# A block-sparse attention and MLP kernel: its planned issue order replaced by a written-out table

## The chip, the cores and the metric

One Trainium2 chip, one of its cores. The metric is the device time of one execution in microseconds (us). The kernel before took 760.85, 762.11 and 762.67 us in three runs, so its median is 762.11 us. A measurement of this kernel can tell a difference of about 0.2%, some 1.5 us, from no change.

## The reference

Four batches, eight heads, 768 positions, head size 64. Attention is restricted by blocks of 32 positions: a query block sees its own block and its two neighbours, the first and the last block, and three drawn blocks. The result is laid out as 3072 tokens of 512 and goes through two matrix products with a gate between them. The weights are float64 (512 by 2048 and 2048 by 512), q, k and v are float32.

```python
scores = np.where(mask, scale * q @ k.T, -1e9)
attn = softmax(scores)
x = (attn @ v).transpose(0, 2, 1, 3).reshape(3072, 512)
h = x @ w_in
g = h * np.tanh(np.log1p(np.exp(np.minimum(h, 20.0))))
out = g @ w_out
```

## The kernel before

Every float32 or float64 operand is brought to a common scale and split into two 16-bit halves, a high part and a low part, and every product is made of three matmuls (high-high, low-high, high-low).

**Weights.** The float64 weights come in as pairs of int32 words. VectorE turns them into float32 with three instructions for each of 8 pieces of w_in (`wi`) and 16 pieces of w_out (`wo`): `add_decode`, L901, L904 and L907. TensorE forms a sum of squares of each piece (`gram_wi`, `gram_wo`, L373), and the scale from it (`gsc`, L1029, for all of w_in) must be there before the first MLP product. `split_i` (L953) then makes the high half on ScalarE or VectorE (L962, L964) and the low half either on VectorE in one instruction (L968) or on GpSimd (POOL) in two (L971, L973).

**Attention.** 52 jobs, 13 for each batch; a job takes two query blocks (or one dense block that sees all keys). `attend` (L698) writes a job as a chain: S, the scores (TensorE, L674, 48 matmuls of 64x32 tiles when the gathered keys are whole, 96 in the first 12 jobs); the maximum (VectorE, L737); the exponentials (ScalarE); T, four transposes (TensorE, L680); the halves `ph` and `pl`; O, the product with v (TensorE, L818, 96 matmuls of 128x32 tiles, 144 in a dense job) into the one bank `obank`; the division by the sum (VectorE, `r` at L837 and `xs` at L840, which read `obank`); X, a transpose back (`tx`, L680, and L870 in the first six jobs); and the halves of x. GpSimd gathers the keys (`kg`, L611) and the SP queue the values (`vg`).

**MLP.** For 12 tiles of 256 tokens: h products (L1068, 12 matmuls to a half task), the gate on ScalarE, VectorE and GpSimd, y products (L1162). The last four tiles use a scheme with seven products instead of eight (L1281). A tile's h products need `gsc` and the x of all the jobs that cover its tokens. For the first tile, h of tile 0, these are jobs 0 to 4.

**The order.** The whole kernel is first listed as 2703 tasks (`Plan.add`, L76): a task names its engine or the engines it may run on, a duration, what it reads and writes, and the buffers it takes. `Plan.emit` (L124) then replays this list against assumed durations: at every step it takes the task that could start first, among those within 0.02 us by urgency (`URGE`, `JOBS`, `PIECES`, L33 to L35), picks an engine for tasks that have a choice, and issues its instructions. Each engine runs its own instructions strictly in the order of issue. `pace` (L1507) holds attention back on TensorE: set starting times for the first 14 jobs, a share of MLP work between jobs after that, and, after 200 us of planned time, at least 2.0 us of MLP work between any two S or O tasks:

```python
if kind in ("S", "O") and start > SPACE[0] and at["done"] < at["dense"] + SPACE[1]:
    late = max(late, SPACE[2])
```

`fill` (L1541) issues products of zeros into an unused part of `obank` (L1545, 240 columns) wherever the plan shows TensorE empty between 14 and 200 us, one for each 0.14 us, unless an O is half done. There are 176 of them.

Of the kernel before, what the change touches and what calls it, by code (L numbers as in the profile page):

```python
# [1 line left out]

# [62 lines left out]
class Plan:  # L65
# [55 lines left out]
                return at + dur if grain is True else min(at + dur, start + grain)  # L121
        return start

    def emit(self, pace, fill):  # L124


        for t in self.tasks:
            t.left = len(t.deps)
            for d in t.deps:
                d.then.append(t)  # L130
        free, ready, dma, held = {}, {}, {}, {}
        lanes = {w: [[0.0] * self.LANES, 0] for w in ("hard", "soft")}

        def open_(t):
            for e in t.ways:
                ready.setdefault(e, []).append(t)

        for t in self.tasks:
            if not t.left:
                open_(t)  # L140
        todo = len(self.tasks)
        self.order = []
        while todo:
            best = None
            load = {e: free.get(e, 0.0) + 0.5 * sum(t.ways[e][0] for t in ts if len(t.ways) == 1)
                    for e, ts in ready.items() if e != "PE"}
            for eng, ts in ready.items():
                f = free.get(eng, 0.0)
                cand = []
                for t in ts:  # L150
                    at, took = t.ready, []
                    for ring, k in t.new:
                        slot = self.room(ring, took)
                        if slot is None:
                            at = None
                            break
                        took.append((ring, slot[1], k))
                        at = max(at, slot[0])
                    if at is None:
                        continue  # L160
                    if len(t.ways) > 1:
                        done = {e: max(at, load.get(e, 0.0)) + x[0] for e, x in t.ways.items()}
                        if done[eng] > min(done.values()):
                            continue
                    if t.kind and t.kind[0] == "dma":
                        lane, n = lanes["soft" if eng == "POOL" else "hard"]
                        at = max(at, lane[n % self.LANES])
                    start = self.port(held, eng, max(at, f), t.ways[eng][2])
                    late, bias = pace(t, start) if eng == "PE" else (0.0, 0.0)
                    cand.append((start + late, t.ready + t.key + bias, t.n, start, t, took))  # L170
                if not cand:
                    continue
                lo = min(c[0] for c in cand)
                c = min((c[1:] for c in cand if c[0] <= lo + 0.02), key=lambda c: c[:2])
                if best is None or c[2] < best[0]:
                    best = *c[2:], eng
            start, t, took, t.eng = best
            for e in t.ways:
                ready[e].remove(t)
            t.dur, fn, port = t.ways[t.eng]  # L180
            if port:
                held[t.eng] = start, t.dur, port
            t.fill = fill(free.get("PE", 0.0), start) if t.eng == "PE" else 0
            end = start + t.dur + (pace(t, None) or 0.0)
            free[t.eng] = end
            if t.kind and t.kind[0] == "dma":

                lane, n, end, t.end = *lanes["soft" if t.eng == "POOL" else "hard"], start, 0.0
                each = t.kind[1] / t.kind[2]
                for k in range(n, n + t.kind[2]):  # L190
                    end = max(end, lane[k % self.LANES]) + t.dur / t.kind[2]
                    other = max([x for e, x in dma.items() if e != t.eng], default=0.0)
                    at = max(dma.get(t.eng, 0.0), end + 0.3)
                    dma[t.eng] = at + each + min(each, 0.5 * max(other - at, 0.0))
                    lane[k % self.LANES] = land = max(dma[t.eng] + 0.5, end + t.lat + min(max(other - end, 0.0), 3.5))
                    t.end = max(t.end, land)
                lanes["soft" if t.eng == "POOL" else "hard"][1] += t.kind[2]
                free[t.eng] = end
            else:
                t.end = end + t.lat  # L200
            t.at = start
            for ring, slot, k in took:
                self.rings[ring][slot] = k
            fn()
            todo -= 1
            self.order.append(t)
            for x in t.then:
                x.left -= 1
                x.ready = max(x.ready, t.end + self.SEM if x.eng != t.eng or t.kind and t.kind[0] == "dma" else t.end - t.lat)
                if not x.left:  # L210
                    open_(x)


def edges(nb, gpc):
# [5 lines left out]
def attn_mish_kernel(ctx: ExitStack, tc: tile.TileContext, qT, kT, v, sampled, blocks, w_in, w_out, out):  # L220
# [13 lines left out]
    B, NPR, D2, S = qT.shape  # L234
# [108 lines left out]
    plan = Plan(RINGS)  # L343
# [843 lines left out]
    dma = lambda d, n=1: ("dma", d, n)  # L1187
# [156 lines left out]
    for b in range(B):  # L1344
        order = [(0,)] + [(q, q + 1) for q in range(1, NB - 1, 2)]
        order.insert(DL, (NB - 1,))
        for qbs in order:
            sus = [{"b": b, "qb": qb} for qb in qbs]
            dense = len(qbs) == 1
            jobs.append({"i": len(jobs), "b": b, "sus": sus, "dense": dense, "nt": S // KT if dense else len(qbs)})  # L1350
    nj = len(jobs)
# [52 lines left out]
    for k in range(NFP):  # L1404
# [3 lines left out]
        key=-9)  # L1408

    order = []  # L1410
# [21 lines left out]
    for i, job in enumerate(jobs):  # L1432
        b, o = job["b"], i % JB
# [61 lines left out]
    for st in order[len(plain):] + [None]:  # L1495
        steps, end = pair_y(prev, st is None)
        ys = [(0.66, x) for x in steps[:-1]] + [(0.66, lambda s_=steps[-1], e=end: (s_(), e()))]
        mixed([(2.62, lambda n=n, st=st: moe_h(st, n, None)) for n in range(NFP)] if st else [], ys)
        prev = st
    total = sum(t.ways["PE"][0] for t in plan.tasks if t.kind and t.kind[0] == "M")  # L1500

    RES, START = 575.0, [26, 134, 14, 98, 36, 170, 29, 37, 53, 110, 67, 166, 3, 46]
    at = {"done": 0.0, "next": 0.0, "job": 0, "last": None, "shape": None, "open": False, "dense": -9.0}

    SPACE = 200.0, 2.0, 1.5

    def pace(t, start):  # L1507

        kind = t.kind[0] if t.kind else None
        if start is None:  # L1510
            shape = 0.0
            if t.eng == "PE":
                now = kind if kind in ("S", "O") else None
                shape, at["shape"] = 0.1 * (now != at["shape"]), now
                if kind == "M":
                    at["done"] += t.dur
                elif kind == "S":
                    at["job"] += 1
                    at["next"] = at["done"] + max(total - at["done"] - RES, 0.0) / max(nj - at["job"], 1)
                elif kind == "O":  # L1520
                    at["open"] = not t.kind[2]
                at["last"] = kind
                if kind in ("S", "O"):
                    at["dense"] = at["done"]
            return shape
        if kind == "M":
            return 0.0, 1e6 - t.ready + t.kind[1] - t.key
        late = 0.0
        if kind == "S":
            i = t.kind[1]  # L1530
            if i < len(START):
                late = max(START[i] - start, 0.0)
            elif at["done"] < at["next"]:
                late = 1.0
        if kind in ("S", "O") and at["last"] in ("S", "O") and kind != at["last"]:
            late = max(late, 0.3)
        if kind in ("S", "O") and start > SPACE[0] and at["done"] < at["dense"] + SPACE[1]:
            late = max(late, SPACE[2])
        return late, 0.0

    def fill(a, b):  # L1541

        n = int((b - a - 0.15) / 0.14) if FILL[0] < a < FILL[1] and not at["open"] else 0
        for _ in range(n):
            nc.tensor.matmul(obank[:, NO:NO + NZ], neg[:, 0], neg.rearrange("p n q -> p (n q)")[:, 0:NZ],  # L1545
                             start=True, stop=True)
        return max(n, 0)

    FILL = 14.0, 200.0
    plan.emit(pace, fill)  # L1550
    pools["lcm"].__exit__(None, None, None)
    pools["cm"].__exit__(None, None, None)


# [40 lines left out]
```

## Time and profile before

| | |
|---|---|
| median of three runs | 762.11 us (760.85 to 762.67) |
| the profiled execution, first to last instruction | 760.4 us |
| TensorE busy | 718.7 us (95%), 13086 matmuls |
| VectorE busy | 580.0 us (76%) |
| ScalarE busy | 575.1 us (76%) |
| GpSimd busy | 350.7 us (46%) |
| products of zeros, L1545 | 26.2 us, 176 of them |

The profiled execution is told by its span of 760.4 us; its time with what lies around the span is not given apart, and the median of the runs is 1.7 us above it. The engines are PE (TensorE), PEld (its weight loads), DVE (VectorE), ACT (ScalarE), POOL (GpSimd) and SP. "issue" marks time in which an engine waited for nothing that the profile shows. [...]

### The profile page before, as it was taken

The page shows a single profiled execution, that of the slowest core. Times are in us where ns is not written, and L with a number is a line of the kernel's source. Part 1 is how long each engine was busy: PE and PEld are TensorE (multiplying, and loading weights), DVE is VectorE, ACT ScalarE, POOL GpSimd, SP SyncE. Part 2 cuts the span into 40 slices and gives each one's busy share as a digit, 9 for nine tenths or more (in the row PEclk, how much of TensorE's full clock was granted, in tenths as well). Part 3 has the DMA queues.
Part 4 walks back from the last instruction along what each step waited for, and adds up shares of the span by engine and source line. Part 5 has one row for each costly group of instructions (what it writes and reads, how often), then busy time and mean ns, then how long its engine had stood idle before and what let it go on. Part 6 is the DMA issues. An engine that isn't in the chain of part 4 may idle for free.

```text
span 760.4 us, 31382 instructions
## 1 busy us (share of the span) xinstructions
PE 718.7 (95%) x13086; PEld 546.5 (72%) x13086; DVE 580.0 (76%) x1007; ACT 575.1 (76%) x905; POOL 350.7 (46%) x415
## 2 busy tenths in 40 slices
PE   5867789999999999999999999999999999999997
PEld 4746677775686777776776667667676778888886
DVE  4989878999878766789777866988775765777674
ACT  3566668889788788879788779787887877677762
POOL 2055744536956444545436642558773511421110
PEclk9998899999999999999999999999999999999999
DMA  9688766543334466174246643733541446000000
GB/s 332 221 273 227 245 198 180 169 107 100 122 95 144 123 184 195 54 222 143 71 117 192 189 136 89 228 100 89 155 129 45 121 115 230 28 2 28 1 27 31
DMA packets 60050, 103.76 MB, mean 136 GB/s; under 512 B 8579, under 2 KB 20868, under 8 KB 59908
## 3 DMA queue, kind: packets, MB, share of 16 engines
q1 hardware_dynamic: 53616, 86.28, 37.9%
q10 hardware_dynamic: 6292, 15.47, 5.9%
q8 instruction: 103, 1.69, 0.9%
q14 instruction: 39, 0.32, 0.1%
HBM read 84.58 MB, written 17.14 MB: 134 GB/s over the span
## 4 chain that ended last, share of the span: by engine, by line
PE 73%; DVE 16%; DMA 5%; issue 2%; ACT 2%; SPq 2%; POOL 1%; DVEq 0%; POOLq 0%; ACTq 0%
PE h_None L1068 25%; PE y L1162 18%; PE yr L1281 8%; PE t L680 6%; PE obank L818 5%; PE s L674 5%; DVE wo L907 2%; PE tx L680 2%; DMA vg<-vd 1%; PE obank L1281 1%; DMA raw_q<-in_q_dram 1%; PE obank L1545 1%; DVE v L504 1%; DVE fr_o L1201 1%; DVE hs_None L1107 1%
## 5 line engine op out<-in xcount | busy, mean ns | idle before, releaser
L1068 PEld LDWEIGHTS <-wi 128*128 128x128 f16 x2304 | 222.8, 98 | 32.4 <-issue 2.5
L1068 PE MATMUL h_None<-xh,wi 128*128 128x256 f16 x1152 | 207.2, 273 | 0.0
L611 POOL COPY kg<-kt 128x256 f16 x255 | 125.7, 527 | 121.6 <-PE s L674 110.8
L1162 PE MATMUL y<-wo,g 128*128 128x512 f16 x672 | 160.9, 379 | 1.0 <-DVE wo L1025 0.8
L1068 PE MATMUL h_None<-xl,wi 128*128 128x256 f16 x576 | 157.0, 273 | 0.0
L1120 POOL TENSOR_TENSOR g<-hs_None,g 128x1024 f16<-128x1024 f32 x36 | 85.0, 2363 | 93.0 <-ACT g L1114 49.9
L1162 PEld LDWEIGHTS <-g 128*128 128x128 f16 x768 | 73.0, 98 | 73.2 <-issue 3.6
L756 ACT ACTIVATE pt<-s,nb,ns 128x256 f32<-128x256 f32 (+1 forms) x208 | 106.2, 583 | 1.1
L1079 ACT ACTIVATE hs_None<-h_None,gsc 128x512 f32<-128x512 f32 x96 | 65.4, 684 | 36.6 <-PE h_None L1068 34.1
L783 DVE SCALAR_TENSOR_TENSOR pl<-t,ph 128x512 f16<-128x512 f32 x99 | 67.0, 685 | 32.7 <-ACT ph L779 32.2
L1107 DVE SCALAR_TENSOR_TENSOR hs_None<-us_None,hs_None 128x1024 f32<-128x1024 f32 x48 | 62.5, 1305 | 28.7 <-ACT us_None L1106 28.6
L779 ACT ACTIVATE ph<-t 128x512 f16<-128x512 f32 x112 | 65.6, 598 | 24.1 <-PE t L680 23.6
L680 PE MATMUL t<-ident,pt 128*128 128x128 f32 x448 | 70.1, 283 | 8.3 <-DVE sc_q L409 3.0
L1103 POOL TENSOR_TENSOR us_None<-us_None 128x1024 f32<-128x1024 f32 x24 | 47.9, 1997 | 53.6 <-DVE us_None L1101 53.6
L1068 PE MATMUL h_None<-xr,wi 128*128 128x256 f16 x576 | 66.5, 273 | 0.0
L680 PEld LDWEIGHTS t<-ident,pt 128*128 128x128 f32 x448 | 51.9, 143 | 20.2 <-issue 8.8
L737 DVE TENSOR_REDUCE mx<-s 128x4 f32<-128x1024 f32 x44 | 53.6, 1219 | 16.4 <-PE s L674 16.2
L818 PEld LDWEIGHTS <-ph 128*32 128x32 f16 x3584 | 48.0, 94 | 19.5 <-issue 14.9
L1098 ACT ACTIVATE us_None<-hs_None,hsc 128x1024 f32<-128x1024 f32 x48 | 55.0, 1147 | 0.3
L1105 ACT ACTIVATE us_None<-us_None 128x1024 f32<-128x1024 f32 x48 | 50.7, 1055 | 2.7 <-POOL us_None L1103 2.3
L818 PE MATMUL obank<-vg,ph 128*32 128x65 f16 (+1 forms) x3200 | 50.6, 196 | 1.4 <-issue 1.2
L1106 ACT ACTIVATE us_None<-us_None 128x1024 f32<-128x1024 f32 x48 | 50.4, 1055 | 0.7
(260 smaller groups left out, 1279.4 us busy)
## 6 DMA issues: line engine op xcount, KB each, us to landing
vg<-vd SPq DMA_DIRECT2D x320, 65.0 KB, 2.7
vg<-vd SPq DMA_DIRECT2D x80, 195.0 KB, 3.1
wr<-in_moe_w_in_dram ACTq DMA_DIRECT2D x8, 1024.0 KB, 7.3
wor<-in_moe_w_out_dram ACTq DMA_DIRECT2D x13, 512.0 KB, 6.1
vd<-v SPq DMA_DIRECT2D x12, 520.0 KB, 3.1
vg<-vd SPq DMA_DIRECT2D x12, 520.0 KB, 4.9
raw_k<-in_k_dram SPq DMA_DIRECT2D x12, 512.0 KB, 5.4
raw_q<-in_q_dram SPq DMA_DIRECT2D x12, 512.0 KB, 4.7
```

Of the source, the lines that this page charges most:

```text
L611: nc.gpsimd.tensor_copy(out=dst, in_=tl["kt", b][:, :, ds(j, BS)])
L680: nc.tensor.matmul(out, src, ident, start=start, stop=stop, is_transpose=True)
L756: ex = lambda o, x, g, w: nc.scalar.activation(out=o, in_=x, func=AF.Exp, bias=nb[:, g, w:w + 1], scale=tl["ns", b, sus[w]["qb"] // TB][:, ...
L779: nc.scalar.activation(out=new(at_, "ph", ("ph", i, j), [P, 2, 2, P], F16), in_=tl["t", i, j], func=AF.Copy, scale=PSC)
L783: nc.vector.scalar_tensor_tensor(out=new(at_, "pl", ("pl", i, j), [P, 2, 2, P], F16), in0=tl["t", i, j], scalar=PSC, in1=tl["ph", i, j], o ...
L818: nc.tensor.matmul(o[cs, w, g, 0:v1 - v0], p[:, k, g, cs], vt[:, k, 2 * c + g, v0:v1], start=j == 0 and g == 0 and k == 0 and n == 0, stop ...
L1068: nc.tensor.matmul(h[:, f2, 0:n].rearrange("p (s q) -> p s q", q=BS), wi[:, fp, w, cc, fs], x[:, s0:s0 + sn, cc], start=f2 == 0 and k == 0 ...
L1079: nc.scalar.activation(out=tl[kq][:, 2 * (fp % 2):2 * (fp % 2) + 2, 0:n], in_=tl[kh][:, :, 0:n], func=AF.Copy, scale=gsc[:, fp:fp + 1])
L1107: add("DVE", 1.32 * c, lambda: nc.vector.scalar_tensor_tensor(out=hs(), in0=us(), scalar=-0.5, in1=hs(), op0=ALU.add, op1=ALU.mult), r=[ku ...
L1120: add("POOL", 2.3 * c, lambda: nc.gpsimd.tensor_tensor(out=g(1), in0=hs(), in1=g(0), op=ALU.subtract), r=[kq, ("gh",) + kp], w=[kp], use=[kg],
L1162: nc.tensor.matmul(tl[ky], tl["g", b, t, k][:, g, f, q], wo_at(fc)[:, w], start=fc == 0 and n == 0, stop=fc == NFC - 1 and n == 2)
L1281: nc.tensor.matmul(R(i), lhs, rhs, start=head and j == n == 0, stop=k == NFC // 4 - 1 and j == 1 and n == 2, skip_group_check=True)
```

## The change

The list scheduler, its times and its pacing rules are taken out. The order stands in a string of 2703 words, `ORDER`; a word is a task's number, a letter where it runs on another than its first engine, and the count of zero products to issue ahead of it. `emit` issues the tasks in that order. The tasks themselves, their instructions and their dependencies are the same.

```diff
-    def emit(self, pace, fill):
...
+    def emit(self, order, fill):
+        done = set()
+        self.order = []
+        for word in order.split():
+            n, way, zeros = re.fullmatch(r"(\d+)([b-z]?)(?:\+(\d+))?", word).groups()
+            t = self.tasks[int(n)]
+            t.eng = list(t.ways)[ord(way) - 97 if way else 0]
+            assert t not in done and t.deps <= done, "the order puts a task before one that it needs"
+            fill(t, int(zeros or 0))
+            t.ways[t.eng][1]()
+            done.add(t)
             self.order.append(t)
...
-    SPACE = 200.0, 2.0, 1.5
-    def pace(t, start):
...
-    def fill(a, b):
-        n = int((b - a - 0.15) / 0.14) if FILL[0] < a < FILL[1] and not at["open"] else 0
+    def fill(t, n):
         for _ in range(n):
+            assert not at["open"]
             nc.tensor.matmul(obank[:, NO:NO + NZ], neg[:, 0], neg.rearrange("p n q -> p (n q)")[:, 0:NZ],
                              start=True, stop=True)
...
-    plan.emit(pace, fill)
+    plan.emit(ORDER, fill)
...
+ORDER = """
+    7 1 0 8 2 9 3 4 53 74 5 6 67 10 85 11 12 14 51 13 15 18 76 16 17 28 92 19 20 22 117b 29 21 61 24 23 75 30+5 93 77
+    99 25 49 54 27 31 32+6 167 26 69 33 34 38 202 64 39 168 192 42 35 56 52 118 169 170 36 119 37 171 60 94 43 62
...
```

What the table moves shows at three places. The numbers in names are buffer numbers, which differ between the two programs.

**First place: TensorE from the last O of job 4 to the first h of the MLP.** `tx_4` is X of job 4, `s_6` the scores of job 6, `t_5` the transposes of job 5. A line of "..." leaves out the repeated weight loads and matmuls of one task. Before:

```order
L818 MATMUL obank_109<-vg1_116,ph_4_1_2529 32x65
...
L1545 MATMUL obank_109<-neg_73 128x240
...
L680 MATMUL tx_4_2777<-ident_64,xs_4_2766 128x128 x2
...
L680 MATMUL t_5_0_2847<-ident_64,pt_5_2780 128x128 x4
...
L870 MATMUL tx_4_2777<-xh_0_0_1180,neg_73 128x128
...
L674 MATMUL s_6_2903<-kt_0_203,q_0_1_1552 32x96
...
L1068 MATMUL h_0_0_0_None_3032<-xh_0_0_1180,wi_71 128x256
```

And now:

```order
L818 MATMUL obank_109<-vg1_116,pl_4_1_2593 32x65
...
L680 MATMUL t_5_0_2757<-ident_64,pt_5_2683 128x128 x4
...
L1506 MATMUL obank_109<-neg_73 128x240
...
L680 MATMUL tx_4_2772<-ident_64,xs_4_2765 128x128 x2
...
L870 MATMUL tx_4_2772<-xh_0_0_1135,neg_73 128x128
...
L674 MATMUL s_6_2797<-kt_0_259,q_0_1_1612 32x96
...
L1068 MATMUL h_0_0_0_None_2950<-xh_0_0_1135,wi_71 128x256
```

Before, 24 zero products stand here (7 ahead of X, 6 between X and the transposes of job 5, 11 ahead of the scores of job 6); now there are 9 (3 ahead of X, 2 and 4 after the scores). Ahead of the first h the same tasks have been issued on TensorE in both, and 169 zeros before against 113, which is all of them, now. The other seven of before stand later, among the products of the first tiles.

**Second place: TensorE at the O of job 18 and the S of job 20.** `obank` is O, `s_20` is S, h is the MLP. Before, S of job 20 stands between two h tasks:

```order
L1068 MATMUL h_1_0_0_None_7946<-xh_1_0_6581,wi_71 128x256
L674 LDWEIGHTS q_1_1_6506
L674 MATMUL s_20_8016<-kg0_113,q_1_1_6506 32x256
...
L674 MATMUL s_20_8016<-kg1_114,q_1_1_6506 32x256
L1068 LDWEIGHTS wi_71
L1068 MATMUL h_1_0_1_None_8069<-xh_1_0_6581,wi_71 128x256
```

And now it follows O of job 18 directly:

```order
L818 LDWEIGHTS pl_18_1_7766
L818 MATMUL obank_109<-vg1_116,pl_18_1_7766 32x65
L674 LDWEIGHTS q_1_1_6693
L674 MATMUL s_20_7912<-kg0_113,q_1_1_6693 32x256
...
L674 MATMUL s_20_7912<-kg1_114,q_1_1_6693 32x256
L680 MATMUL t_19_0_7981<-ident_64,pt_19_7781 128x128 x4
```

After the first h task an S and an O stand side by side nowhere in the order before, and at 36 places now (31 with S first). An S or O comes right after another kind of work 97 times before and 56 times now, and is followed by another kind 97 times and 56 times.

**Third place: the low halves of w_in, on VectorE and GpSimd, at the piece `wr_6`.** Before, GpSimd's order has, between the key gathers:

```order
L611 COPY kg1_114<-kt_0_203 128x8x32
L535 TENSOR_TENSOR q_0_1_1552<-raw_q_0_1_570,q_0_1_1552 128x1024
L971 TENSOR_SCALAR wi_71<-wi_71,ws_2_1299 128x1024
L973 TENSOR_TENSOR wi_71<-wi_71 128x1024
L580 TENSOR_LOAD offk_86
```

Now VectorE has one of these low halves itself, at L968:

```order
L388 SCALAR_TENSOR_TENSOR gram_q_0_1_677,ss_q_0_1_1173<-gram_q_0_1_677,ident_64 128x128
L901 TENSOR_SCALAR wi_71<-wr_6_890 128x1024
L968 SCALAR_TENSOR_TENSOR wi_71<-wi_71,ws_0_1095 128x1024
L904 SCALAR_TENSOR_TENSOR wi_71<-wr_6_890,wi_71 128x1024
L737 TENSOR_REDUCE mx_2_1332<-s_2_1191 128x4
```

Before, five of the eight low halves were GpSimd's; now all eight are VectorE's, four of the five ahead of the division of job 4. Three key gathers of the early jobs go from GpSimd to ScalarE. Over the whole kernel 96 tasks that may run on two engines change theirs: GpSimd loses 21 tasks, ScalarE gains 12, VectorE 5 and SP's queue 4.

## Rows read from the trace of the kernel before

**Rows 1.** The page: the span, and the granted clock in 40 slices.

```profile
span 760.4 us, 31382 instructions
...
PEclk9998899999999999999999999999999999999999
```

**Rows 2.** Busy time by stretch: PE, PEld, DVE, ACT, POOL, then PEclk, DMA.

```profile
20.00:94.00 74.00, 55.94 (x1486) 44.71 (x1484) 65.86 (x116) 45.72 (x87) 34.65 (x36) 0.88 0.77 238
...
200.00:400.00 200.00, 199.79 (x3954) 142.55 (x3952) 154.16 (x275) 166.64 (x281) 104.86 (x141) 1.00 0.48 138
```

**Rows 3.** The groups of instructions in 20 to 94 us: the zeros.

```profile
L1545 PE MATMUL obank<-neg 128*128 128x240 f16 x157 | 22.4, 289 | 3.2 <-DVE xs L840 3.2
```

**Rows 4.** The chain that ended last, 20 to 94 us, shares by line.

```profile
by line: PE obank L1545 10.8%; DMA wr<-in_moe_w_in_dram 7.4%; issue 6.8%; PE t L680 6.7%; PE s L674 6.7%; DVE wi L904 5.8%; SPq L580 5.5%; DVE wi L901 5.3%; DVE wo L907 4.8%; DMA vg<-vd 3.8%; DVE v L504 3.4%; DVE wi L968 3.4%; DVE wi L907 3
```

**Rows 5.** The same chain, 84 to 94 us, in order of time: start, us, what.

```profile
86.44 1.56 PE obank L1545 x7
...
88.42 1.20 PE obank L1545 x6
...
90.69 1.68 PE obank L1545 x11
```

**Rows 6.** Groups in 20 to 94 us: the low halves of w_in by engine.

```profile
L973 POOL TENSOR_TENSOR wi<-wi 128x1024 f16<-128x1024 f32 x4 | 8.9, 2221 | 0.3
...
L968 DVE SCALAR_TENSOR_TENSOR wi<-wi,ws 128x1024 f16<-128x1024 f32 x3 | 4.0, 1326 | 0.0
```

**Rows 7.** VectorE's timeline, 43 to 66 us: start, us, engine, line.

```profile
44.16 2.59 DVE L901 TENSOR_SCALAR wi<-wr 128x1024 int32<-128x1024 int32 x1 [0.92 <-DMA wr<-in_moe_w_in_dram]
...
52.42 0.85 DVE L901 TENSOR_SCALAR wi<-wr 128x1024 int32<-128x1024 int32 x1
...
63.86 3.03 DVE L907 SCALAR_TENSOR_TENSOR wo<-wr,wo 128x1024 int32<-128x1024 int32 x1
```

**Rows 8.** GpSimd's timeline in the same stretch.

```profile
44.09 2.12 POOL L973 TENSOR_TENSOR wi<-wi 128x1024 f16<-128x1024 f32 x1
...
63.68 2.13 POOL L973 TENSOR_TENSOR wi<-wi 128x1024 f16<-128x1024 f32 x1
```

**Rows 9.** TensorE's waits, 94 to 200 us: total, times, longest (first and last of six).

```profile
PE obank L818 <- issue: 3.6, 3, 1.2
...
PE gram_wo L373 <- DVE wo L907: 0.3, 1, 0.3
```

**Rows 10.** TensorE's waits from 200 us to the end (first and last of four).

```profile
PE t L680 <- DVE xl L867: 1.3, 1, 1.3
...
PE obank L818 <- issue: 0.5, 1, 0.5
```

**Rows 11.** TensorE's timeline: an S between two h tasks.

```profile
220.74 0.27 PE L1068 MATMUL h_None<-xh,wi 128*128 128x256 f16 x1
220.94 0.85 PE L674 MATMUL s<-kg,q 64*32 64x256 f16 x48
221.73 0.28 PE L1068 MATMUL h_None<-xh,wi 128*128 128x256 f16 x1
```

**Rows 12.** TensorE's timeline: the start of an O and of the h after it.

```profile
339.40 0.25 PE L818 MATMUL obank<-vg,ph 128*32 128x65 f16 x8
...
340.34 0.28 PE L1068 MATMUL h_None<-xh,wi 128*128 128x256 f16 x1
```

**Rows 13.** TensorE's timeline: the end of the S of job 5, and an O.

```profile
84.08 0.20 PE L674 MATMUL s<-kt,q 64*32 64x96 f16 x1 [1.91 <-issue]
84.09 0.27 PE L674 MATMUL s<-kg,q 64*32 64x160 f16 x8
84.28 0.25 PE L818 MATMUL obank<-vg,ph 128*32 128x65 f16 x8
```

**Rows 14.** DMA queues: the one that carries TensorE's instructions.

```profile
q8 instruction: 103, 1.69, 0.9%
```

**Rows 15.** The chain that ended last, 150 to 160 us: a dense job's O.

```profile
154.94 1.39 PE obank L818 x144
```

More of the change, by code (lines that the diff above doesn't have):

```diff
@@ L1 @@
+import re
 from contextlib import ExitStack
@@ L122, in port @@
         return start
-    def emit(self, pace, fill):
[L127 to L141, printed above, removed]
-        self.order = []
[L143 to L205, printed above, removed]
-            self.order.append(t)
[L207 to L211, printed above, removed]
@@ new lines, in emit @@
+    def emit(self, order, fill):
+        done = set()
+        self.order = []
+        for word in order.split():
[6 more added lines that the diff above has]
+            done.add(t)
+            self.order.append(t)
+        assert len(done) == len(self.tasks), "the order leaves tasks out"
@@ L1499, in attn_mish_kernel @@
         prev = st
-    total = sum(t.ways["PE"][0] for t in plan.tasks if t.kind and t.kind[0] == "M")
-    RES, START = 575.0, [26, 134, 14, 98, 36, 170, 29, 37, 53, 110, 67, 166, 3, 46]
-    at = {"done": 0.0, "next": 0.0, "job": 0, "last": None, "shape": None, "open": False, "dense": -9.0}
-    SPACE = 200.0, 2.0, 1.5
-    def pace(t, start):
[L1509 to L1539, printed above, removed]
@@ L1541, in fill @@
-    def fill(a, b):
-        n = int((b - a - 0.15) / 0.14) if FILL[0] < a < FILL[1] and not at["open"] else 0
+    at = {"open": False}
+    def fill(t, n):
         for _ in range(n):
+            assert not at["open"]
             nc.tensor.matmul(obank[:, NO:NO + NZ], neg[:, 0], neg.rearrange("p n q -> p (n q)")[:, 0:NZ],
                              start=True, stop=True)
-        return max(n, 0)
-    FILL = 14.0, 200.0
-    plan.emit(pace, fill)
+        if t.kind and t.kind[0] == "O":
+            at["open"] = not t.kind[2]
@@ L1556 @@
+"""
 def kernel(**inputs):
```

93 lines of the change are left out of this document (added), and 17 rows, old and new, of the table ORDER.

## The prediction

> **What bounds the kernel now.** I read the page first, then busy time by stretch, then the chain and the waits of the stretches in which TensorE is not full.
>
> From 200 us on TensorE has no room: it is busy 199.79 of the 200 us from 200 to 400 [rows 2], and from 200 us to the end only four kinds of wait are listed, 1.3 + 0.8 + 0.7 + 0.5 = 3.3 us [rows 10]. What an order can give there is little idle time, but it can still make the work itself shorter. From 94 to 200 us six kinds of wait add up to 3.6 + 0.8 + 0.7 + 0.7 + 0.4 + 0.3 = 6.5 us [rows 9].
>
> The loss lies ahead of the first MLP product. From 20 to 94 us TensorE counts 55.94 us busy, but 22.4 of these are zeros [rows 2, 3], and VectorE is busy 65.86 of 74 us: it decodes weights and takes part in each attention job. So this stretch is VectorE's, with 8.1 us of idle time on it. The granted clock is 0.88 there and 1.00 after [rows 2].
>
> The first h product can't be moved ahead by work on TensorE: the same tasks precede it in both orders. Its start, and the density after it, are what can change.
>
> **The change, part by part.**
>
> *The start of the MLP.* Four more low halves of w_in come to VectorE ahead of the division of job 4. Each takes 1.33 us there (mean 1326 ns), against 2.22 us for the second of the two instructions on GpSimd [rows 6]: +5.3 us of VectorE. Against that stands what GpSimd did to VectorE: the L901 that begins at 44.16 takes 2.59 us beside an L973 that runs from 44.09 to 46.21, and 0.85 us where none runs; the L907 at 63.86 takes 3.03 us beside the L973 at 63.68 [rows 7, 8]. Two such stalls of 1.74 us go: -3.5 us. So VectorE has +1.8 us more to do before the division. Then come the zeros. At the end of this stretch 7, 6 and 11 of them stand in the chain itself between the division of job 4 and the first h: 1.56 + 1.20 + 1.68 = 4.44 us [rows 5], 0.185 us each; the nine that remain cost 1.67, so -2.8 us. Last, VectorE's 8.1 us of idle time: the new order mixes decoding and attention in another way, S of job 0 ahead of the first decoding among them; I take a quarter of it, -2.0. Together -3.0 us. Ends: if no stall goes and no zero was really in the way, +5.3; if VectorE lost all its idle time, it could come -8 us earlier.
>
> *94 to 200 us.* The 3.6 us of "issue" waits will move rather than go (below). Of the other 2.9 us I take half, -1.5. Ends 0 and -6.5. The seven later zeros, 7 x 0.14 us, lie in these waits and I give them nothing. If VectorE is late with w_out here, the first y products wait: it is behind by the 1.8 us above at most, and TensorE has three more half h tasks, 1.3 us each, ahead of the first y than before, so that cover holds.
>
> *S beside O.* This is the largest part, and it lies where TensorE is full, so each tenth of a microsecond counts. From the last h matmul to the first of S is 0.20 us, against 0.11 from h to h; from the last h to the first after S is 0.99 us [rows 11]. So an S between two h tasks costs 0.99 - 0.11 = 0.88 us. An O takes 0.94 us from its first matmul to the next h [rows 12], with the same way in 0.20 + 0.94 - 0.11 = 1.03 us. Side by side: S of job 5 and O of job 4 are one of the two such pairs before, and there O begins 0.19 us or less after the last matmul of S [rows 13]; h follows S after 0.20. If S to O cost those 0.20 us, a pair would be 0.20 + 0.79 + 0.94 - 0.11 = 1.82 us against 1.91 apart; if it cost no more than h to h (0.11), 1.73. I take 0.13 us of gain for a pair, nearer to the full cost because the row is: 36 x 0.13 = -4.7 us, ends -3.2 and -6.5.
>
> *What a pair may cost.* S and O are short matmuls, so a pair is 144 matmuls and 144 weight loads in under 2 us, where an h task has 48 in 2.6 us. The queue q8 brought 103 packets [rows 14] for 26,172 matmuls and loads: 254 in each. And three O tasks between 94 and 200 us stop in their middle with nothing to wait for, 3.6 us in all, up to 1.23 each; the S of job 5 does so for 1.91 us [rows 9, 13]. I read these as TensorE having run through a packet's worth before the next was there. After 200 us, where the order before held S and O at least 2.0 us of MLP apart, there is one such wait, of 0.5 us [rows 10]. A pair has 288 instructions. That is also what a dense job's O has, and one ran its 144 matmuls in 1.39 us unbroken [rows 15]. So it doesn't always happen. I take two pairs in 36 at 1.2 us: +2.5 us, ends 0 and every second pair, +22. [...]
>
> *After 200 us otherwise.* 96 tasks have another engine. ACT is busy 166.64 and DVE 154.16 of the 200 us from 200 to 400 [rows 2], so a moved task of 1 or 2 us finds room, and GpSimd gives work away. Waits of the size of today's 3.3 us will stand at other places: 0, ends -3.3 and +6.
>
> Sum: -3.0 - 1.5 - 4.7 + 2.5 = -6.7 us. The profiled span was 760.4 us [rows 1]; the median of the runs lies 1.7 us above. I set the change against the median: 762.1 - 6.7 = **755.4 us**.
>
> **The rivals.**
>
> *The order closes the gaps too* (0.16). VectorE loses most of its idle time (-8), half of the waits behind 94 us go (-3 and -1.7), no pair stalls: -8 - 3 - 4.7 - 1.7 = -17.4, 744.7 us. For it: VectorE's waits before 94 us are on what other engines could have done earlier. Against it: the orders differ little there.
>
> *Pairs starve TensorE* (0.13). The one that ends slower. Place: inside or right behind an S-O pair, in the full stretch, where nothing hides it. At 1.2 us a stall it takes back the other 9.2 us once eight pairs stop, more than one in five; at one in three, 14.4 us, the time is 762.1 - 9.2 + 14.4 = 767.3. For it: the waits above, all in dense work, and that the order before kept S and O apart after 200 us. Against it: the dense O's.
>
> *VectorE pays for the moved halves* (0.10). No stall goes, since other GpSimd work (L535, L1103, L1120) remains to collide with: +5.3 - 2.8 = +2.5 at the start, nothing at 94 to 200: 762.1 + 2.5 - 4.7 + 2.5 = 762.4, no change.
>
> *Fewer zeros, lower clock* (0.05). [...]
>
> **How the numbers follow.** The forecast has 0.56. Faster by over 0.2% (1.5 us, what a measurement here can tell) are the gaps' case and nearly all of the forecast's, 0.70; within 0.2% the moved halves, some of the clock's case and the upper end of the forecast, 0.12; slower the starved pairs, the rest of the clock's case and bad waits after 200 us, 0.18. The range goes from 745, the gaps' case, to 766, short of one pair in three stopping; about 0.09 is left out above and 0.06 below. The forecast's own range is 750 to 760.
>
> **What would show it.** Right: the first h starts 1 to 5 us earlier than before; after 200 us S to O takes 0.16 to 0.20 us; TensorE's "issue" waits after 200 us stay under 4 us; VectorE's L901, L904 and L907 beside L973 are gone. Wrong: "issue" waits of 10 us or more in L674 and L818 after 200 us (starved pairs); a first h no earlier than before with VectorE busy 90% ahead of it (moved halves); a granted clock under 0.80 from 20 to 94 us (zeros); a first y that waits for `wo` for more than 2 us.

## The result, and the profile after

The changed kernel took 754.23 us (median of six runs, 751.58 to 757.15) beside 761.48 us for the kernel before on the same chip: a ratio of 0.9899, with a 95% interval of 0.9872 to 0.9926, so 1.0% faster. The forecast was 755.4 us. The time is right; its terms are not all right, and that two of the errors cancelled is luck.

The page of the changed kernel answers to [rows 1] and [rows 14]:

```profile
span 752.6 us, 31176 instructions
...
PE 708.4 (94%) x13023; PEld 543.4 (72%) x13023; DVE 548.1 (73%) x1015; ACT 579.3 (77%) x927; POOL 281.7 (37%) x380
...
PEclk9889899999999999999999999999999999999999
...
q8 instruction: 102, 1.67, 0.9%
```

TensorE's busy time fell by 10.3 us, and the span by 7.8. Busy time by stretch, in the columns of [rows 2]:

```profile
20.00:94.00 74.00, 50.18 (x1380) 38.93 (x1378) 59.64 (x121) 47.58 (x98) 13.91 (x21) 0.86 0.78 241
94.00:200.00 106.00, 102.56 (x2042) 79.20 (x2040) 87.05 (x158) 94.56 (x153) 52.57 (x59) 0.98 0.47 148
...
200.00:400.00 200.00, 196.67 (x4074) 142.71 (x4073) 142.95 (x274) 162.17 (x278) 95.36 (x142) 1.00 0.46 140
```

From 20 to 94 us VectorE is busy for 59.64 of 74 us, where it had 65.86 [rows 2]. Had VectorE set the pace there, the first h would have come earlier. It starts where it did. TensorE's timeline there:

```profile
93.31 0.60 PE L680 MATMUL t<-ident,pt 128*128 128x128 f32 x4
93.74 0.27 PE L1068 MATMUL h_None<-xh,wi 128*128 128x256 f16 x1
```

Before, it started at 93.75. So in these two profiles nothing of the 7.8 us was won ahead of it. TensorE's waits, 94 to 200 us and from 200 us to the end, answer to [rows 9, 10]:

```profile
PE obank L818 <- issue: 1.9, 1, 1.9
PE t L680 <- ACT pt L756: 1.4, 1, 1.4
...
PE h_None L1068 <- issue: 3.2, 4, 1.0
PE t L680 <- DVE pl L783: 0.5, 2, 0.3
PE obank L818 <- issue: 0.5, 2, 0.3
PE t L680 <- issue: 0.3, 1, 0.3
PE obank L818 <- DMA vg<-vd: 0.3, 1, 0.3
```

In the first stretch 6.5 us became 3.3; in the second 3.3 became 4.8, and of these 4.0 are "issue", 0.5 before.

**Where the 7.7 us behind the first h went.** From the first h on TensorE is nearly full, and does the same products in both orders, but for the seven zeros of before. So I took each matmul's step from the start of the one ahead of it, and grouped the steps by what stands on both sides. A kind's usual step is its median in both kernels.

| from the first h to the last matmul, us | before | after |
|---|---|---|
| usual steps into, out of and between S and O | 38.8 | 28.2 |
| usual steps between all other tasks | 66.4 | 73.2 |
| usual steps inside tasks | 509.3 | 509.3 |
| above the usual, to 200 us | 15.1 | 10.2 |
| above the usual, from 200 us | 32.8 | 33.9 |
| sum, with the last matmul's own 0.3 | 662.7 | 655.0 |

S and O side by side gave 10.6 us of steps and cost 6.8 at others: -3.8. The stretch to 200 us gave -4.9. Behind it nothing was won: +1.1.

### The profile page after: what moved, and what is told of

Its sections match the earlier page's. It is cut to its first block, busy times and chain, and to the rows that moved or that the text cites. A ratio compares the mean times of both kernels' runs of the same rounds, so it can differ in the third digit from the quotient of the medians.

```text
span 752.6 us, 31176 instructions
## 1 busy us (share of the span) xinstructions
PE 708.4 (94%) x13023; PEld 543.4 (72%) x13023; DVE 548.1 (73%) x1015; ACT 579.3 (77%) x927; POOL 281.7 (37%) x380
## 4 chain that ended last, share of the span: by engine, by line
PE 82%; DVE 7%; DMA 4%; issue 3%; SPq 2%; ACT 1%; POOLq 0%; ACTq 0%; POOL 0%; DVEq 0%
PE h_None L1068 31%; PE y L1162 21%; PE yr L1281 8%; PE obank L818 6%; PE t L680 6%; PE s L674 5%; DMA vg<-vd 2%; PE obank L1281 1%; PE tx L680 1%; DMA raw_k<-in_k_dram 1%; DVE hs_None L1107 1%; DMA raw_q<-in_q_dram 1%; SPq L580 1%; DVE v L504 1%; ACT pt L756 1%
## 5 line engine op out<-in xcount | busy, mean ns | idle before, releaser
L611 POOL COPY kg<-kt 128x256 f16 x246 | 112.5, 491 | 163.2 <-PE s L674 146.3
L1162 PE MATMUL y<-wo,g 128*128 128x512 f16 x672 | 159.1, 379 | 0.0
L1120 POOL TENSOR_TENSOR g<-hs_None,g 128x1024 f16<-128x1024 f32 x36 | 81.0, 2251 | 131.3 <-ACT g L1114 85.7
L818 PEld LDWEIGHTS <-ph 128*32 128x32 f16 x3584 | 47.8, 94 | 14.7 <-issue 12.9
L818 PE MATMUL obank<-vg,ph 128*32 128x65 f16 (+1 forms) x3200 | 49.1, 196 | 2.6 <-issue 2.3
L818 PEld LDWEIGHTS <-pl 128*32 128x32 f16 x1792 | 46.5, 96 | 5.7 <-issue 3.8
```

Of the source, the lines that this page charges most:

```text
L611: nc.gpsimd.tensor_copy(out=dst, in_=tl["kt", b][:, :, ds(j, BS)])
L818: nc.tensor.matmul(o[cs, w, g, 0:v1 - v0], p[:, k, g, cs], vt[:, k, 2 * c + g, v0:v1], start=j == 0 and g == 0 and k == 0 and n == 0, stop ...
L1120: add("POOL", 2.3 * c, lambda: nc.gpsimd.tensor_tensor(out=g(1), in0=hs(), in1=g(0), op=ALU.subtract), r=[kq, ("gh",) + kp], w=[kp], use=[kg],
L1162: nc.tensor.matmul(tl[ky], tl["g", b, t, k][:, g, f, q], wo_at(fc)[:, w], start=fc == 0 and n == 0, stop=fc == NFC - 1 and n == 2)
```

## The experiments

Each kernel was compared with the kernel before on the same chip; e1 to e4 ran on one chip, e5 to e8 on a second and e9 to e12 on a third, so ratios are compared across these groups, and times within one. "First h" is where it starts in the profiled run, "since" the time from there to the last matmul's end, "issue" the sum of TensorE's issue waits behind 94 us.

| run | median us | ratio to before, 95% interval | first h | since | issue |
|---|---|---|---|---|---|
| kernel before | 761.5 to 763.2 | 1 | 93.75 | 662.7 | 4.8 |
| the change | 754.23 | 0.9899 (0.9872 to 0.9926) | 93.74 | 655.0 | 5.9 |
| e1 pairs apart | 765.34 | 1.0036 (1.0016 to 1.0056) | 96.22 | 663.2 | 2.8 |
| e2 shift 88 | 781.21 | 1.0236 (1.0199 to 1.0272) | 95.29 | 676.3 | 24.7 |
| e3 shift 212 | 753.04 | 0.9857 (0.9823 to 0.9892) | 94.99 | 652.5 | 3.8 |
| e4 loads on SP | 756.91 | 0.9927 (0.9900 to 0.9954) | 96.32 | 656.6 | 9.6 |
| e5 19 zeros fewer | 751.95 | 0.9855 (0.9831 to 0.9879) | 95.21 | 650.7 | 3.8 |
| e6 narrow zeros | 754.40 | 0.9878 (0.9854 to 0.9902) | 92.83 | 657.8 | 8.7 |
| e7 late part alone | 751.48 | 0.9844 (0.9821 to 0.9868) | 92.31 | 655.9 | 9.1 |
| e8 early part alone | 765.68 | 1.0038 (1.0021 to 1.0056) | 95.11 | 664.7 | 1.7 |
| e9 late part, shifted | 750.18 | 0.9824 (0.9787 to 0.9862) | 92.75 | 650.2 | 4.6 |
| e10 late part, narrow zeros | 754.00 | 0.9890 (0.9856 to 0.9924) | 96.13 | 650.1 | 3.3 |
| e11 both loads on SP | 754.08 | 0.9879 (0.9848 to 0.9909) | 93.59 | 655.2 | 6.9 |
| e12 halves on GpSimd | 753.22 | 0.9889 (0.9849 to 0.9930) | 91.24 | 654.2 | 6.6 |

### Where in the program the gain lies (e7, e8)

The two orders were joined at the first h: e7 has the words of the order before up to there and then those of the change, e8 the reverse. The sets of tasks ahead of it are nearly the same, so the join moves 4 or 10 tasks.

```diff
         for _ in range(n):
             assert not at["open"]
-            nc.tensor.matmul(obank[:, NO:NO + NZ], neg[:, 0], neg.rearrange("p n q -> p (n q)")[:, 0:NZ],
-                             start=True, stop=True)
+            at["zeros"] = at.get("zeros", 0) + 1
+            parts = 3 if at["zeros"] <= 34 else 1
+            for c in range(parts):
+                nc.tensor.matmul(obank[:, NO:NO + NZ // parts], neg[:, 0],
+                                 neg.rearrange("p n q -> p (n q)")[:, 0:NZ // parts], start=True, stop=True)
```

(28 in place of 34 in e8.)

> The order of the kernel before up to the first h, then the order of the change; 34 of the zeros cut in three so that the late part's instructions stand at the same places against the boundaries as in the change. Theory A (nothing is gained ahead of the first h, 7.7 us behind it): as the change, 753 to 756. Theory D (the new early table is what lets the stretch from 94 to 200 us run without waits, for the weights it has decoded by then): that stretch keeps its 6.5 us of waits, 757 to 760.

> The order of the change up to the first h, then the order of the kernel before; 28 zeros cut in three, so that the late part's instructions stand where they stood before. Theory A: no gain, 760.5 to 763.5, with the waits between 94 and 200 us as before (6.5 us). Theory D: 757 to 759, with these waits halved.

The late part alone is 1.6% faster than the kernel before, and its interval ends below that of the whole change. The early part alone is 0.2 to 0.6% slower. So the new order's late words bring the gain, and its early words cost. In the six profiled runs with the new early order (the change, e1, e2, e3, e5, e8; zeros cut or fewer in some) the first h starts at 93.74 to 96.22, 95.1 on average; in the three with the old one (before, e7, e9) at 92.31 to 93.75, 92.9. In e8 the waits between 94 and 200 us are 7.2 us, about the 6.5 of before: the new early table doesn't clear that stretch, the late one does. Theory A was right about the late part and wrong about the early: it is not worth nothing, it costs some 3 us (0.38%). Not all of that is shown to arise ahead of the first h: of e8's 3.4 us over the kernel before in the profile, 1.4 stand ahead of it and 2.0 behind, where TensorE waits 3.4 us for value gathers between 94 and 200 us.

### The places of the stalls (e2, e3, e5, e9)

In the change the issue wait after the S at 254.22 falls into the h behind it. TensorE's timeline:

```profile
254.22 0.84 PE L674 MATMUL s<-kg,q 64*32 64x256 f16 x45
254.99 0.66 PE L680 MATMUL t<-ident,pt 128*128 128x128 f32 x4
...
255.92 0.27 PE L1068 MATMUL h_None<-xl,wi 128*128 128x256 f16 x1
257.19 0.39 PE L1068 MATMUL h_None<-xh,wi 128*128 128x256 f16 x2 [1.00 <-issue]
```

Number all records that TensorE has in the trace (weight loads, matmuls and its sequencer's own) in order of time, and the eight such stalls from 117 us on end with 4290, 8897, 9666, 10946, 14529, 15298, 18114 and 21442 records ahead of them. By then q8 has brought 16, 34, 37, 42, 56, 59, 70 and 83 packets of 16384 bytes. Less 256 records for each packet, 193 or 194 are left every time: one and the same place in every packet, called a boundary here. (The 249 in e2's expectation comes from a count with fewer records.) The three stalls ahead of the first h and all eight of the kernel before stand at the same place. Each in the change resumes 2.2 to 2.8 us after the last packet's transfer began, and no transfer there began more than 293 records ahead of its boundary. So two things stand at each stall of this trace: a boundary, and records just ahead of it that run through faster than the next packet comes. To move the boundaries and nothing else, zeros were cut into three:

```diff
-            nc.tensor.matmul(obank[:, NO:NO + NZ], neg[:, 0], neg.rearrange("p n q -> p (n q)")[:, 0:NZ],
-                             start=True, stop=True)
+            at["zeros"] = at.get("zeros", 0) + 1
+            parts = 3 if at["zeros"] <= 22 else 1
+            for c in range(parts):
+                nc.tensor.matmul(obank[:, NO:NO + NZ // parts], neg[:, 0],
+                                 neg.rearrange("p n q -> p (n q)")[:, 0:NZ // parts], start=True, stop=True)
```

(22 in e2, 53 in e3. In e5 the last 19 zeros are taken out instead; in e9 it is the joined order of e7 with 25.)

> The changed kernel with the first 22 zero products cut into three of 80 columns each: the same columns, but every later TensorE instruction stands 88 places further on in its queue (44 products and 44 weight loads). Theory A (stalls fall where a boundary, every 249 of the instructions counted here, comes right behind a short dense stretch): the stalls of the changed kernel at 238.97, 255.92, 289.16, 380.61, 481.30 and 560.49 us leave their places and others come, by my reckoning some 12 us of them in place of 5 to 7: +5 to +9 us, 759 to 763. Theory B (the stalls belong to the tasks, not to the place in the queue): the same stalls at the same tasks, and no change, 753 to 756.

> The same with the first 53 zero products cut in three: later instructions stand 212 places further on. Theory A: with this shift hardly any boundary falls behind a dense stretch, the stalls after 125 us shrink from about 5 us to 1, and those at 65, 85 and 117 us go too: -4 to -6 us, 748 to 750. Theory B: no change, 753 to 756; and if cutting zeros costs by itself, slower, as the run with 22 would be too.

> The changed kernel without the last 19 of its 113 zero products, which stand between 72 and 95 us; every later TensorE instruction then stands 38 places further ahead, about where the shift by 212 put it against the boundaries. Theory A (the boundaries' places decide the stalls): the issue waits behind 94 us fall from 5.9 to 4 or less, as in the run shifted by 212, and without that run's cut zeros: 749 to 752, as fast as that run or faster. Theory C (the zeros hold the clock, and their number is what counts): the granted clock from 20 to 94 us falls under 0.82 and the time rises to 755 or more.

> The late part alone again (the old order up to the first h, the new one behind it), with 25 zeros cut in three in place of 34, so that the late part's instructions stand 212 places further on than in the change, where the stalls were fewest. Theory A: of its 9.1 us of issue waits behind 94 us about 4 are left; 746 to 749, faster than both kernels. Theory B (places in the queue don't matter where the early part is the old one): 750 to 753.

TensorE's waits of e2, from 94 to 200 us (first line) and from 200 us on, then the longest but one in its timeline:

```profile
PE s L674 <- issue: 5.2, 2, 2.8
...
PE h_None L1068 <- issue: 9.4, 4, 3.5
PE obank L818 <- issue: 7.8, 5, 2.2
PE s L674 <- issue: 1.4, 2, 0.9
PE y L1162 <- issue: 0.5, 1, 0.5
PE t L680 <- issue: 0.4, 1, 0.4
```

```profile
273.61 0.27 PE L1068 MATMUL h_None<-xl,wi 128*128 128x256 f16 x1
277.10 0.61 PE L1068 MATMUL h_None<-xh,wi 128*128 128x256 f16 x2 [3.22 <-issue]
```

The same columns of zeros, the same order, 88 instructions more ahead: 24.7 us of issue waits in place of 5.9, and 781 us. Of the 22.8 us between the spans of the two profiled runs, 18.8 are these waits. All of e2's stalls stand in the same place of a packet as those of the change (193 or 194), at other tasks. Theory A stands, though its reckoning of some 12 us was half of what came, and its 759 to 763 us were missed by far. The other way, e3 and e5 both come to 3.8 us, by two different edits; five profiles in which TensorE has the change's own instructions at the change's own places (the change, e4, e6, e11, e12) have 5.9 to 9.6. Both are faster than the change by 0.4%, with intervals that still touch its own, and e3's 753.04 us alone would fit theory B too. In e5 the granted clock from 20 to 94 us fell to 0.80 and the time fell too, against theory C. And e9 joins the two findings: the old early order, the new late one, boundaries at the better place. Its waits from 200 us on:

```profile
PE h_None L1068 <- issue: 1.2, 2, 1.0
PE s L674 <- issue: 0.8, 1, 0.8
PE t L680 <- DVE pl L783: 0.7, 2, 0.4
PE obank L818 <- issue: 0.6, 2, 0.4
```

At 750.18 us it is 1.8% faster than the kernel before and beats the change too (0.9787 to 0.9862 against 0.9872 to 0.9926), though it stayed above the 746 to 749 expected. Against e7, which is the same order with other boundaries, the intervals overlap: there the issue waits, 9.1 and 4.6 us, show the gain and the times don't.

### The pairs pulled apart (e1)

At 33 places one MLP task was put between S and O, 17 times by moving the second of the two back, 16 times the MLP task that stood ahead of the first. For S of job 27 and O of job 25 (969 is the O, 1951 an h):

```diff
-    1012 990 988 1933 969 1029 1031 991 1951
+    1012 990 988 1933 1029 1031 991 1951 969
```

> The changed kernel with the 33 S-O pairs after 200 us pulled apart again: in each, one MLP task is put between the two, with nothing else moved. Theory A (a pair saves one change of tile shape, and its 288 short instructions cost stalls at the packets of TensorE's instructions): 33 x 0.10 = +3.3 us come back as changes of shape, and the issue waits of about 4 us after 200 us, which stand right behind pairs, go to under 1: net -1 us, 753 to 755. Theory B (the pairs are worth the 4.7 us of the prediction and the stalls have nothing to do with them): +3.3 to +4.7, 757.5 to 759, with the issue waits still there.

Neither: 765.34 us, 11 more than the change. Both parts of theory A are there. The usual steps rose by 3.1 us (S and O +7.6, others -4.5), 0.094 for a pair, and the issue waits after 200 us went from 4.0 to 1.0. What no theory had is in TensorE's waits from 200 us on:

```profile
PE t L680 <- DVE pl L783: 2.7, 4, 1.4
PE obank L818 <- DMA vg<-vd: 1.8, 4, 0.8
PE tx L680 <- DVE xl L867: 1.4, 1, 1.4
PE tp_q L396 <- ACT I-6388_6389 L364: 0.9, 1, 0.9
```

S or O one MLP task later, or that task earlier, makes transposes, divisions and gathers late: 8.7 us of waits that are not issue, where the change has 0.8. The first h, too, came 2.5 us later than in the profile of the change, from the same order. So e1 prices the change of tile, and is no price of pairs as a whole.

### What holds the early part (e4, e11, e12, e6, e10)

VectorE's stalls beside GpSimd are gone as predicted. Its decoding of w_in in the change, 20 to 94 us (min/median/max in ns), against the 2.59 and 3.03 us of [rows 7]:

```profile
L901 DVE TENSOR_SCALAR wi<-wr x7: 682/687/694, 24.5 to 68.1; 128x1024 int32<-128x1024 int32 x7
L907 DVE SCALAR_TENSOR_TENSOR wi<-wr,wi x7: 1212/1217/1220, 28.1 to 71.2; 128x1024 int32<-128x1024 int32 x7
```

But VectorE now waits, most for TensorE's squares of w_in, and TensorE for ScalarE (from the waits of 20 to 94 us):

```profile
DVE gram_wi L388 <- PE gram_wi L373: 6.4, 2, 4.2
...
PE t L787 <- ACT ph L779: 5.5, 4, 4.2
PE t L680 <- ACT pl L792: 4.4, 1, 4.4
```

ScalarE does this meanwhile (its timeline):

```profile
38.61 0.42 ACT L608 ACTIVATE kg<-kt 128x256 f16 x1 [0.24 <-issue]
42.80 0.37 ACTq L893 DMA_DIRECT2D wr<-in_moe_w_in_dram  x1
43.23 1.15 ACT L962 ACTIVATE wi<-wi,ws 128x1024 f16<-128x1024 f32 x1 [4.20 <-DMA vg<-vd]
...
50.87 0.40 ACTq L893 DMA_DIRECT2D wr<-in_moe_w_in_dram  x1
51.32 0.60 ACT L779 ACTIVATE ph<-t 128x512 f16<-128x512 f32 x1 [4.61 <-DMA vg<-vd]
```

Two weight loads (L893, pieces wr_4 and wr_7) wait on ScalarE's queue until a value gather has landed, and the halves and exponentials stand behind them, 4.2 and 4.6 us. Before, ScalarE waited for no DMA in this stretch.

```diff
-    153
-    135
+    153b
+    135b
```

That is e4; e11 and e12 are:

```diff
-    129
-    153
+    129b
+    153b
```

```diff
-    108
-    128
-    144
-    146
-    164
+    108b
+    128b
+    144b
+    146b
+    164b
```

(153 is the load of wr_7, 135 of wr_5, 129 of wr_4; "b" is SP for a load and GpSimd for a low half.)

> The changed kernel with two weight loads (the pieces wr_7 and wr_5) issued on SP's queue at the same places of the order, not on ScalarE's. Theory A (the first h product did not come earlier because ScalarE stood 3.8 and 4.6 us behind these two loads, which waited for a value gather to land, with ph, nb and pt queued behind): ScalarE's two waits for DMA vg go, TensorE's waits for ph (5.5 us) and pl (4.4 us) ahead of 94 us shrink by half or more, the first h starts 2 to 4 us earlier, 750 to 752. Theory B (something else held the start, or SP's gathers are now late by as much): the first h at 93 to 95 us, 753 to 757.

> The changed kernel with the two weight loads that ScalarE waited 4.2 and 4.6 us for (pieces wr_4 and wr_7) on SP's queue; the run before with loads on SP had moved wr_7 and wr_5, and so only one of the two. Theory G (these two waits are why the new early part is no faster than the old): ScalarE's waits for DMA vg go, and the first h comes to 91 to 93 us from a mean of 95 over the five runs with the new early part and whole zeros; 751 to 753. Theory H (the early part is a loop of engines in turn, and one wait taken out reappears elsewhere): the first h at 94 to 97, 754 to 758.

e4 moved the wrong pair: the first of the two waits stayed, and the first h came at 96.32. e11 moved the right one, and ScalarE's waits from 20 to 94 us begin with:

```profile
ACT pt L756 <- issue: 8.3, 1, 8.3
```

Its timeline shows what stood ahead of it:

```profile
58.50 0.37 ACTq L893 DMA_DIRECT2D wr<-in_moe_w_in_dram  x1
58.93 1.02 ACT L756 ACTIVATE pt<-s,nb,ns 128x256 f32<-128x256 f32 x2 [8.28 <-issue]
```

That is the third load, wr_5, with one wait of 8.3 us in place of two of 8.8. Theory H: the wait reappeared at the next load. The first h at 93.59 is within what the same order gave by itself.

> The changed kernel with five low halves of w_in back on GpSimd, as before (L971 and L973 in place of L968). Theory F (they are what the new early part pays for, 5 x 1.33 us of VectorE): the first h 2 to 3 us earlier, 751 to 753. Theory A (VectorE waits 15 us there anyway, and L973 beside VectorE's instructions stretches these again, 1.7 us each): the first h as late or later, 754 to 758.

With the five halves back on GpSimd the first h came earliest of all, at 91.24, which is theory F. The time says less: 0.9889 against 0.9899, no difference by the intervals. Whether the halves cost something stays open. ScalarE still waits 4.2 us behind the second of the two loads there, so that wait alone doesn't set the first h.

One thing differs between all these profiles that no edit here holds fixed: the stalls at packet boundaries ahead of the first h, which the table's column leaves out. They come to 4.3 us before, 3.6 in the change, 8.2 in e4, 0.6 in e6, 1.6 in e12 and none in e11. The chain of the change, 84 to 94 us, has one right ahead of the first h, in the O of job 4:

```profile
84.34 0.85 PE obank L818 x80
85.19 2.07 issue
87.25 0.35 PE obank L818 x9
```

In the new early order the three profiles with under 2 us of them have the first h at 91.24 to 93.59, the seven others at 93.74 to 96.32. So they are a rival of the loads and of the halves that these runs don't part from them.

e6 and e10 leave every zero in its place at 16 columns (10 adds e9's cuts):

```diff
-            nc.tensor.matmul(obank[:, NO:NO + NZ], neg[:, 0], neg.rearrange("p n q -> p (n q)")[:, 0:NZ],
+            nc.tensor.matmul(obank[:, NO:NO + 16], neg[:, 0], neg.rearrange("p n q -> p (n q)")[:, 0:16],
```

> The changed kernel with every zero product 16 columns wide in place of 240: the same number of instructions, so no boundary moves, but next to no work in them. Theory C (the zeros' work holds the clock): the granted clock from 20 to 94 us falls from 0.86 to 0.7 or less, the first h starts 2 to 5 us later, 756 to 760. Theory A (the early stretch hangs on DMA landings, ScalarE and VectorE, so the zeros' work buys little): the first h at 93 to 97 us, 753 to 756.

> The same kernel with every zero product 16 columns wide, the number of instructions kept. Theory A (as in the changed kernel, the zeros' work buys nothing, and in the old early order 8 us of the chain ahead of the first h were zeros): the granted clock from 20 to 94 us falls, but the first h starts no later than 93 us; 745 to 749. Theory C (here, where TensorE's zeros are denser, they do hold the clock): the first h 2 us later or more, 750 or more.

Busy time from 20 to 94 us of e6, of e9 and of e10 (the first number behind the engines is the granted clock, as a share of full speed):

```profile
20.00:94.00 74.00, 51.13 (x1423) 39.90 (x1408) 60.69 (x121) 49.27 (x100) 11.79 (x22) 0.77 0.79 236
```

```profile
20.00:94.00 74.00, 54.82 (x1517) 44.95 (x1515) 63.54 (x117) 45.81 (x86) 38.00 (x35) 0.93 0.76 236
```

```profile
20.00:94.00 74.00, 47.95 (x1425) 38.20 (x1422) 62.32 (x115) 45.50 (x86) 34.04 (x32) 0.72 0.76 233
```

In the new early order the clock fell from 0.86 to 0.77 and nothing got slower: theory A. In the old one it fell from 0.93 to 0.72, the first h moved from 92.75 to 96.13, and since then the two kernels are equal to 0.1 us (650.2 and 650.1): theory C. The intervals of the whole time still touch (e10 from 0.9856, e9 to 0.9862), but on their common chip each of e10's six runs took longer than each of e9's (from 751.84, to 751.7 us). So the zeros' work is worth some 4 us in the old order and nothing that these runs can tell in the new. Why it differs isn't shown; that TensorE is in the chain of the old order and not of the new would explain it.

## Why the prediction was right, point by point

**The start of the MLP, -3.0: wrong.** The step that failed is "Together -3.0 us". Its pieces on VectorE came true (no stall beside L973, VectorE 59.64 us busy), but I read the stretch as VectorE's, and counted the loads that move on ScalarE's queue at nothing. What the runs show in its place: VectorE has 6.2 us less to do there and the first h still starts at 93.74 us, so the stretch isn't VectorE's alone. Two of the loads wait 8.8 us, TensorE waits for ScalarE, and VectorE for TensorE. By e8 the new early part costs 0.2 to 0.6%. That the loads' waits are this cost is not shown: in e11 they only changed place, and the stalls at packet boundaries ahead of the first h are a rival. The cause stays open.

**94 to 200 us, -1.5: right for the waits it counted, too small in all.** The steps above the usual fell by 4.9 us. Of the 2.9 us of other waits 1.4 are left, as forecast; the first y no longer waits for `wo`. But the 3.6 us of issue waits in O, of which I wrote that they "will move rather than go", came to 1.9, and the other 1.7 us are in no wait that the view lists. This belongs to the late table (e7 keeps it, e8 hasn't got it).

**S beside O, -4.7: the right mechanism, somewhat too large.** From S to O is 0.20 us, no less than from S to h. S and then O in the change, against the 0.79 us from S to h in [rows 11]:

```profile
341.01 0.85 PE L674 MATMUL s<-kg,q 64*32 64x256 f16 x48
341.79 0.25 PE L818 MATMUL obank<-vg,ph 128*32 128x65 f16 x8
```

The saving for a pair is then one change into a tile shape, 0.20 - 0.11 = 0.09 us, which e1 gave back as 0.094; I had taken 0.13. An S or O comes right after another kind of work 41 times less than before (56 against 97), and 41 x 0.094 makes 3.9, the -3.8 of the table. The steps show a cost at each change of tile shape, by unlike amounts: 0.199 us from S to O, where no full-size matmul lies between, but 0.126 from O to S and 0.128 from O to h, against 0.109 from h to h.

**Pairs starving TensorE, +2.5: right in kind and near in size, wrong in place.** The issue waits after 200 us rose from 0.5 to 4.0, +3.5, mostly in the first h task behind a pair, so that watching L674 and L818 alone would have missed 3.2 of them. What the step left out is that the size hangs on where the boundaries happen to lie: 4.0 us in the change, 19.5 in e2. The rival "pairs starve TensorE" is not what happened and is what would have happened with 44 more products and loads ahead: e2 is 2.4% slower than the kernel before. My 0.13 for it was a chance on an alignment, which the count of instructions in the order could have told in part. Most boundaries pass without a stall: of the change's 102 packets 11 have one. Behind the first h it costs up to 3.5 us (e2).

**After 200 us otherwise, 0: wrong in the small.** Other waits went from 2.8 to 0.8 us, -2.0.

Together, by the table: -3.8 - 4.9 + 1.1 = -7.6 behind the first h and 0 ahead of it, where the forecast had -3.7 behind and -3.0 ahead. The gain of 94 to 200 us filled the place of the one that failed.

Of the other rivals, the gaps' case came true in part (waits behind 94 us), and not at the start. The clock with fewer zeros was 0.86 against 0.88 (0.83 in e1, whose early order is the same), and in e6 even 0.77 costs nothing that the times show. In e6 and e10 narrower zeros went with a lower clock (0.86 to 0.77 and 0.93 to 0.72), and in e10 alone with a later first h, by 3.4 us.

## What to carry to other kernels

Where TensorE is full, put the tasks of small tiles side by side and count the times that it comes to them from full-size work: 41 fewer at 0.09 us are 4 us here. When a program is dense with short matmuls, see where its issue waits stand against the packets of its instructions before two orders are compared, since 88 cheap instructions ahead of the dense part made this kernel 3.4% slower. Before a DMA issue goes to a compute engine's queue, see what it will wait for: here two of them on ScalarE's queue waited for a landing, 4.2 and 4.6 us with all behind them, and when both were moved to SP's queue the next load had a wait of 8.3 us.

## What the runs showed that I had not expected

- An alignment of TensorE's instructions is worth more than the whole change: 88 instructions moved the time by 27 us, with issue waits of 24.7 us against 5.9.
- Every such stall stands in the same place of a packet (193 or 194 records past a multiple of 256, in the kernel before, the change, e2, e3, e7 and e9) and ends 2.2 to 2.9 us after the packet's transfer began, whatever the task.
- The change and e1, which have the same instructions up to there, had their first h at 93.74 and 96.22 us. One profile of that stretch can't tell 2 us.
